# Reordered reloads, stored swapped spectra and moved bulk loads in a fused forward and backward kernel

## Chip, core and metric

The program runs on one NeuronCore of one Trainium2 chip. The metric is device microseconds for one execution of the whole program; the figure compared is the median of several executions.

## What is computed

A model of four residual layers, A, B, A, B, and all its gradients, for one sequence of S = 2048 positions and D = 448 channels in bf16:

```
x = A_q
x = x + A(layernorm(x), k, v, shift_k, ssm_k, ssm_D)
x = x + B(layernorm(x), w1, w2)
x = x + A(...)            # the same k, v, kernels
x = x + B(...)            # the same w1, w2

A(q, ...): k_shift = 4-tap causal convolution of k;  kv = k_shift * v
           y = irfft(rfft(kv, 4096) * rfft(ssm_k, 4096))[:2048] + kv * ssm_D
           return q * y
B(x, w1, w2): silu(x @ w1) @ w2,   w1 is 448 x 1792, w2 is 1792 x 448
```

The outputs are x and the gradients for q, k, v, shift_k, ssm_k, ssm_D, w1 and w2. Neither k, v nor the convolution kernels depend on x, so y is the same in both A layers and is computed once.

## The kernel before, in words

**Prefix** (`_ssm_prefix`). Two long transforms of length 4096, one of `ssm_k` and one of `kv`, are made as two stages of matrix products on TensorE: `_fft_stage1` with the constant M1 (128 x 16 x 2 x 128, 1 MB in bf16), transposes, then a second stage with the 128 x 128 constant `Gsb`. The real and imaginary parts of a spectrum lie in the two halves of the partitions (0 to 63 and 64 to 127). A complex product therefore needs two elementwise products: `pa` is spectrum times spectrum, `pb` is one spectrum times the other *with its halves swapped*. Both are then combined by TensorE with two constants (`GiA`, `GiB`, or their conjugate forms `GiAc`, `GiBc`). The two spectra are stored to DRAM as `SPEC_d["K"]` and `SPEC_d["KV"]` for the gradient.

**Main** (`Main.run`). The sequence is worked in four chunks c of 512 positions. Layers are numbered L = 0 (first B) and L = 1 (second B). The forward part runs chunk by chunk; each half of B's hidden layer (7 blocks of 128 features) is made by `h`. For L = 0, `h` stores the pre-activations to DRAM as `DT_d` and the activations, transposed, as `A_d[0]`. Four of the 14 feature blocks (`W2_PLAIN`) take another way: they go to DRAM as they are (`AP_d`), and `turn_plain(i)` later reads one block back through a transposing DMA and stores it.

- The *second loop over c for L = 1* does, for each chunk, `g_pre` (load and transpose the incoming gradient), the second half of `h`, `out`, then `ga`, and at the end `gn`.
- The *loop over c for L = 0* does the same backward part for the first B layer. Its silu slopes come from the stored pre-activations: `load_d(c, half)` reloads one 896 KB tile `dTl`, and `slope` turns it in place with ScalarE.
- `ga` makes, in seven steps `fp`, the product `ps_g` on TensorE, a copy `ghp` on ScalarE, and `ghT` = slope times `ghp` on VectorE. After step 3 the first half of `ghT` is complete, after step 6 the second: each is handed to `store_turned`, which issues two transposing DMAs and leaves the store to `GH_d` to the next call (`flush`).
- `gn` makes `ps_n` = `ghT` times w1 transposed and the backward of both layer norms, on VectorE for the greater part (`ln_bwd`). It writes `gYb`, the gradient of y.

All transposing DMAs, the reloads `dTl`, the loads `nb_l` and `na_l` (`load_n`) and the weight-gradient loads `dstat` are issued by SyncE (SP), in one queue and in order.

Buffers that matter: tag `D` has three slots for `dT` and `dTl`; a reload takes the slot that the `ghT` products just finished with. Tag `WA` holds w1 and later `GO` (the whole incoming gradient, 1.8 MB); tag `WB` holds w2 and later `mov3` (1.8 MB).

**Suffix** (`_ssm_suffix`). The transform of `gYb` (stage 1 with M1, reloaded as `M1s`; transposes into `Zg`), then seven pairs of chunks: `spectrum(cp)` makes the second stage for 2048 columns and loads the stored spectra `kk_c`; `inverse(cp)` makes `pa`, `pb` for both stored spectra and the inverse second stage `ps_v`. `spectrum(cp + 1)` is called before `inverse(cp)`. Then come the inverse first stage with `Minvs`, the elementwise products with `ksf` (the shifted k) and `gks` (v), and the gradients of k, v and the convolution kernels.

**Weight gradients** (`_gw2`, `_gw1`). 56 jobs: each loads a 512 KB tile `dstat` (from `A_d` or `GH_d`) and makes 16 matmuls `ps_d` against a moving matrix: `X`, `GO`, `mov3` or `mov1`. They stand last in the program.

**Order.** The framework's scheduler gives each engine one fixed order of instructions, made ahead from program order as priority, dependencies, buffer slots and a model of durations. Instructions that stand late in the program, the `ps_d` jobs above all, are put where the model finds an engine free. `issue_after(x)` keeps the instructions of a block behind x on their engine. On the chip each engine follows its order and waits on semaphores.

Of the kernel before, what the change touches and what calls it, by code (L numbers as in the profile page):

```python
# [13 lines left out]
ALU = mybir.AluOpType  # L14
# [19 lines left out]
def make_fft_consts():  # L34
# [44 lines left out]
    GiBc = np.roll(GiBc, 64, axis=0)  # L79
# [169 lines left out]
def _pm(ap2d):  # L249
    return ap2d.rearrange("(p j) d -> p j d", j=J)  # L250
# [213 lines left out]
class Main:  # L464
# [98 lines left out]
    def h(self, c, L, nT, half, hold):  # L563
# [3 lines left out]
        hold.append((aT, dT))  # L567
        for ft0, n, at in ((0, 2, 1), (2, 2, 0), (4, 2, None), (6, 1, None)) if half == 0 else ((7, 1, None), (8, 2, 1), (10, 2, 0), (12, 2, None)):
# [20 lines left out]
        if L == 1:  # L589
            self.store_turned(k.A_d[1], aT, c, half)  # L590

# [24 lines left out]
    def ga(self, c, L, gT, dT, mid=None):  # L616
        nc, k = self.nc, self.k
        ghT = [self.td.tile([P, NF // 2, 512], BF16, name=f"ghT{h}", tag="T", bufs=3) for h in range(2)]
        for fp in range(NF // 2):
# [12 lines left out]
            if fp in (3, 6):  # L632
                hh = (fp - 3) // 3
                self.store_turned(k.GH_d[L], ghT[hh], c, hh)
        return ghT
# [71 lines left out]
    def run(self):  # L707
# [21 lines left out]
        for c in range(4):  # L729
            gb, gT = self.g_pre(c, 1)  # L730
            self.h(c, 1, nT, 1, cur)
# [3 lines left out]
            self.turn_plain(c)  # L735
            if c == 3:
                d0 = self.load_d(0, 0)
                self.slope(d0)
                k.GO = k.wk.tile([P, NT, D], BF16, name="GO", tag="WA")
                with self.tc.issue_after(k.d_load.ins):  # L740
                    nc.sync.dma_start(out=k.GO[:], in_=_pm(k.grad_out[0]))
            box = []
            ghT = self.ga(c, 1, gT, cur, (lambda: box.append(self.b_pre(c + 1, 3))) if c < 3 else None)
# [5 lines left out]
            else:  # L749
                d1, e0 = self.load_d(0, 1), self.load_d(1, 0)  # L750
# [5 lines left out]
        for c in range(4):  # L756
# [3 lines left out]
            ghT = self.ga(c, 0, gT, dT, (lambda: self.slope(e0)) if c < 3 else None)  # L760
            if c < 3:
                d0, d1 = e0, self.load_d(c + 1, 1)
                if c < 2:
                    e0 = self.load_d(c + 2, 0)
                gn = self.g_pre(c + 1, 0)
            self.gn(c, 0, ghT, nb, lambda tl: self.X[:, 4 * c + tl, :], na)
            if c < 3:
                with self.tc.issue_after(k.d_load.ins):
                    nl = self.load_n(c + 1)
        self.flush()  # L770
# [53 lines left out]
def _ssm_suffix(k):  # L824
# [7 lines left out]
    with ExitStack() as es:  # L832
        pool = lambda name: es.enter_context(tc.tile_pool(name=name, bufs=1, reuse_waits="tile"))
        sp0 = pool("sp0")
        k.M1sb = sp0.tile([P, 16, 2, P], BF16, name="M1s", tag="kk0")
        with tc.high_priority():
            nc.gpsimd.dma_start(out=k.M1sb[:].rearrange("p a c k -> p (a c k)"), in_=k.m1_h.ap())
# [5 lines left out]
        k.mov3 = k.wk.tile([P, NT, D], BF16, name="mov3", tag="WB")  # L843
        ksf = k.yk.tile([P, J, D], BF16, name="ksf", tag="Y")
        B1k = A1[:].rearrange("p a c n s -> p (a c n s)").rearrange("p (q d) -> p q d", d=D)
        _load_minv(k, nc.gpsimd)
        for n2 in range(16):
            _fft_stage1(k, n2, k.gYb[:, n2, :], A1, psum)
        with tc.tile_pool(name="sspec2", bufs=1, reuse_waits="tile") as p1:
# [8 lines left out]
            def spectrum(cp):  # L858
                lo, hi = cp * 2048, (cp + 1) * 2048
                kk = (sp0.tile([P, 2, 2048], BF16, name="kk_c", tag="kk0") if cp % 2 else p1.tile([P, 2, 2048], BF16, name="kk_c", tag="kk1"))  # L860
                xsw = p1.tile([P, 2048], BF16, name="xsw_c", tag="xsw", bufs=2)
                t = [kk[:, 0, :], kk[:, 1, :], xsw]
                nc.gpsimd.dma_start(out=t[0], in_=k.SPEC_d["K"][:, lo:hi])
                nc.gpsimd.dma_start(out=t[1], in_=k.SPEC_d["KV"][:, lo:hi])
                if cp == 4:
                    nc.gpsimd.dma_start(out=k.mov3[:], in_=_pm(k.N_d[3][:]))
                if cp == 2:
                    nc.gpsimd.dma_start(out=ksf[:], in_=_pm(k.KS_d[:]))
# [6 lines left out]
                _swap_halves_dma(k, t[2], Zf, lo, hi, nc.scalar, dlo=0)  # L875
                return t

            def inverse(cp, t):
                for u in range(2):
                    ci = 2 * cp + u  # L880
                    o = slice(u * 1024, (u + 1) * 1024)
                    for spec_t, B1, cnd in ((t[1], B1k, True), (t[0], Z, False)):
# [148 lines left out]
```

## Time and profile before

| what | value |
|---|---|
| time, median of 3 runs | 791.22 us (789.21 to 795.2) |
| the profiled execution: time / span in the profile | 794.11 us / 792.3 us |
| TensorE (PE) busy | 724.7 us, 91% |
| VectorE (DVE) busy | 515.6 us, 65% |
| ScalarE (ACT) busy | 440.6 us, 56% |
| GpSimd (POOL) busy | 101.7 us, 13% |
| mean granted TensorE clock | 0.973 |
| DMA | 183.69 MB, mean 232 GB/s |

Stages by the trace: the prefix to about 100 us; the forward part and L = 1 backward to about 410; L = 0 backward (`dTl` slopes from 404) to 527 on TensorE and to about 550 on VectorE; the suffix's first stage from 532, its spectrum pairs from 568 to about 636; the remaining products to 784.

How to read the rows: PE is TensorE's matmuls, PEld its weight loads, SPq and POOLq the DMA-issuing queues. A row of the timeline is start, duration, engine, line, instruction, and in square brackets the idle time before it and what ended it. A DMA row's duration is that of its issue, not of its transfer. A row of the waits is the waiting instruction, what released it, and the total, number and longest of the waits. "idle" of an engine that isn't on the path costs nothing. In the tables of stretches the last three columns are granted clock, busy share of the DMA engines and GB/s.

### The profile page before, as it was taken

The page shows a single profiled execution, that of the slowest core. Times are in us where ns is not written, and L with a number is a line of the kernel's source. Part 1 is how long each engine was busy: PE and PEld are TensorE (multiplying, and loading weights), DVE is VectorE, ACT ScalarE, POOL GpSimd, SP SyncE. Part 2 cuts the span into 40 slices and gives each one's busy share as a digit, 9 for nine tenths or more (in the row PEclk, how much of TensorE's full clock was granted, in tenths as well). Part 3 has the DMA queues.
Part 4 walks back from the last instruction along what each step waited for, and adds up shares of the span by engine and source line. Part 5 has one row for each costly group of instructions (what it writes and reads, how often), then busy time and mean ns, then how long its engine had stood idle before and what let it go on. Part 6 is the DMA issues. An engine that isn't in the chain of part 4 may idle for free.

```text
span 792.3 us, 12745 instructions
## 1 busy us (share of the span) xinstructions
PE 724.7 (91%) x5025; PEld 381.3 (48%) x5025; DVE 515.6 (65%) x1056; ACT 440.6 (56%) x551; POOL 101.7 (13%) x169
## 2 busy tenths in 40 slices
PE   6999779999999999999978899996989998999995
PEld 4976534444444434434433343343556674545553
DVE  3789778788435978859457976985365625797110
ACT  4879867766466676876836866633536644000000
POOL 1133212222100010000000000010111022111111
PEclk9999989999999999999998999997989999999998
DMA  9359999999968869889998887995978766587660
GB/s 317 136 158 283 373 258 299 308 249 233 254 173 171 174 185 218 218 174 221 356 266 231 213 239 205 247 195 219 397 223 263 244 266 218 173 307 220 192 179 17
DMA packets 188888, 183.69 MB, mean 232 GB/s; under 512 B 135482, under 2 KB 164030, under 8 KB 187804
## 3 DMA queue, kind: packets, MB, share of 16 engines
q1 hardware_dynamic: 173664, 120.93, 59.2%
q0 software_dynamic: 12832, 53.92, 19.8%
q10 hardware_dynamic: 2332, 8.03, 3.2%
q8 instruction: 39, 0.64, 0.3%
q14 instruction: 21, 0.17, 0.1%
HBM read 76.50 MB, written 65.87 MB: 180 GB/s over the span
## 4 chain that ended last, share of the span: by engine, by line
PE 33%; DVE 21%; issue 20%; ACT 13%; DMA 8%; POOL 3%; SPq 0%; POOLq 0%; DVEq 0%; ACTq 0%
PE ps_h L518 5%; PE ps_d L778 5%; PE ps_o L598 4%; PE ps_g L518 4%; PE ps_n L666 3%; DVE dT L113 3%; DMA dTl<-DT_d 3%; ACT ghp L625 3%; DVE lb_junk L641 2%; DMA kk_c<-spec_KV 2%; DVE lb_u L652 2%; PE ps_v L232 2%; DVE ghT L630 2%; PE ps_v L233 2%; ACT na L274 2%
## 5 line engine op out<-in xcount | busy, mean ns | idle before, releaser
L778 PEld LDWEIGHTS <-dstat 128*128 128x128 bf16 x896 | 87.0, 99 | 87.4 <-issue 8.3
L518 PE MATMUL ps_g<-gT,w2T 128*128 128x512 bf16 (+1 forms) x448 | 100.7, 385 | 17.6 <-ACT ghp L625 17.0
L518 PE MATMUL ps_h<-nT,w1sb 128*128 128x512 bf16 (+1 forms) x448 | 103.9, 385 | 4.7 <-DVE dT L113 2.6
L666 PE MATMUL ps_n<-w1T,ghT 128*128 128x448 bf16 x448 | 94.2, 356 | 0.7 <-ACT lb_u L668 0.2
L598 PE MATMUL ps_o<-w2sb,aT 128*128 128x448 bf16 x448 | 90.8, 353 | 0.8 <-ACT aT L574 0.8
L778 PE MATMUL ps_d<-mov,dstat 128*128 128x448 bf16 x448 | 87.2, 352 | 0.9 <-DMA mov<-N_d 0.9
L574 ACT ACTIVATE aT<-ps_h 128x1024 bf16<-128x1024 f32 (+1 forms) x64 | 58.3, 917 | 37.6 <-PE ps_h L518 28.8
L113 DVE CAST dT<-ps_h 128x1024 bf16<-128x1024 f32 (+1 forms) x56 | 59.3, 1066 | 26.2 <-ACT aT L574 26.1
L518 PEld LDWEIGHTS <-w2T 128*128 128x128 bf16 (+1 forms) x448 | 36.3, 97 | 78.1 <-issue 47.3
L625 ACT CAST ghp<-ps_g 128x1024 bf16<-128x1024 f32 x56 | 56.5, 1008 | 30.6 <-DVE ghT L630 18.5
L518 PEld LDWEIGHTS <-w1sb 128*128 128x128 bf16 (+1 forms) x448 | 36.3, 97 | 68.3 <-issue 40.3
L666 PEld LDWEIGHTS <-ghT 128*128 128x128 bf16 x448 | 42.2, 98 | 45.4 <-issue 4.6
L598 PEld LDWEIGHTS <-aT 128*128 128x128 bf16 x448 | 42.1, 98 | 43.4 <-issue 4.3
L778 PE MATMUL ps_d<-X,dstat 128*128 128x448 bf16 x224 | 54.3, 372 | 5.1 <-DMA dstat<-A_d 5.1
L804 ACT COPY do<-ps_dt 112x512 bf16<-112x512 bf16 x14 | 8.2, 585 | 82.6 <-PE ps_dt L802 82.6
L232 PE MATMUL ps_v<-Gsb,pa 128*128 128x128 bf16 x336 | 43.2, 223 | 10.1 <-DVE Zg L113 5.8
L778 PE MATMUL ps_d<-GO,dstat 128*128 128x448 bf16 x224 | 50.0, 355 | 0.0
L233 PE MATMUL ps_v<-Gsb,pb 128*128 128x128 bf16 x336 | 42.2, 223 | 1.0 <-DVE pb L443 0.7
L819 DVE CAST dout<-ps_d 128x448 bf16<-128x448 f32 x14 | 8.7, 622 | 51.4 <-PE ps_d L778 51.4
L232 PEld LDWEIGHTS <-pa 128*128 128x128 bf16 x336 | 33.5, 100 | 11.7 <-DVE pa L442 6.3
L668 ACT ACTIVATE lb_u<-ps_n,rstd 128x448 f32<-128x448 f32 x32 | 20.2, 632 | 33.4 <-DVE X L653 12.1
L630 DVE TENSOR_TENSOR ghT<-dT,ghp 128x1024 bf16<-128x1024 bf16 (+1 forms) x32 | 19.5, 620 | 27.6 <-ACT ghp L625 27.6
(188 smaller groups left out, 1184.8 us busy)
## 6 DMA issues: line engine op xcount, KB each, us to landing
GH_d<-turned SPq DMA_DIRECT2D x16, 896.0 KB, 6.2
dstat<-A_d SPq DMA_DIRECT2D x28, 512.0 KB, 7.2
dstat<-GH_d SPq DMA_DIRECT2D x28, 512.0 KB, 3.8
A_d<-turned SPq DMA_DIRECT2D x12, 896.0 KB, 4.8
DT_d<-dT POOLq DMA_DIRECT2D x8, 896.0 KB, 6.3
dTl<-DT_d SPq DMA_DIRECT2D x8, 896.0 KB, 6.6
spec_K<-Z POOLq DMA_DIRECT2D x7, 512.0 KB, 7.5
KB<-Z POOLq DMA_DIRECT2D x14, 256.0 KB, 12.3
```

The costliest lines, as they stand in the source:

```text
L113: eng.tensor_copy(out, in_)
L232: nc.tensor.matmul(pv[:, i, :], lhsT=pa[:, i * P:(i + 1) * P], rhs=k.Gsb[:, ga, :], start=True, stop=False)
L233: nc.tensor.matmul(pv[:, i, :], lhsT=pb[:, i * P:(i + 1) * P], rhs=k.Gsb[:, gb, :], start=False, stop=True)
L274: nc.scalar.activation(n_g[:, tl, :], src(tl), ACT.Identity, bias=nmr[:, tl:tl + 1], scale=r[:, tl:tl + 1])
L518: self.nc.tensor.matmul(ps[:, u, :], lhsT=w[lo:hi, b, f:f + P], rhs=x[lo:hi, b, :], start=(seen[u] == 1), stop=(seen[u] == ND))
L574: last = nc.scalar.activation(a, ps[:, 0:n, :], ACT.Silu)
L598: nc.tensor.matmul(po[:, :D], lhsT=aT[ft // 7][0][:, ft % 7, tl * P:(tl + 1) * P], rhs=self.w2sb[:, ft, :], start=(ft == 0), stop=(ft == N ...
L625: k.last_gh = nc.scalar.copy(gh[:], ps[:])
L630: nc.vector.tensor_tensor(out=ghT[hh][:, o:o + len(u), :], in0=dT[hh][1][:, o:o + len(u), :], in1=gh[:, u[0]:u[0] + len(u), :], op=ALU.mult)
L666: nc.tensor.matmul(pn[:, :D], lhsT=ghT[ft // 7][:, ft % 7, tl * P:(tl + 1) * P], rhs=self.w1T[:, ft, :], start=(ft == 0), stop=(ft == NF - 1))
L668: last_u = nc.scalar.activation(u0[:], pn[:, :D], ACT.Identity, scale=k.rstd[2 * L + 1][:, t:t + 1], accum_out=cp[:, tl, 0:1])
L778: i = k.nc.tensor.matmul(ps[:, :D], lhsT=st[:, t, :], rhs=mov[:, t, :], start=start and t == 0, stop=stop and t == NT - 1)
```

## The change

Main. The reloads of pre-activations move ahead of transposes on SP's queue: `d0` is loaded at the start of the last `h` of L = 1, and `ga` takes a pair `loads`, of which each is issued just before `store_turned` of its half. Two plain turns each are made in c = 0 and 1, none in c = 2 and 3. `GO` is loaded at the end of c = 0 of the last loop instead of in c = 3 of the loop before. `M1s` is loaded by SP in c = 2 of the last loop, into w2's buffer, instead of by GpSimd into a pool of the suffix at its beginning.

Suffix. The halves are no longer swapped on the fresh spectrum `Zg` (two DMAs from ScalarE's queue per pair, after the second stage's copies). Instead each stored spectrum is loaded twice, once as it is and once with its halves swapped, six DMAs from GpSimd's queue per pair, into a tile of four instead of two parts with two slots. The row rotation of the constant `GiBc` that undid the other swap is dropped. `Minvs`, `ksf` and `gks` are loaded behind the second pair's spectra, `mov3` behind the last pair's.

```
-    GiBc = np.roll(GiBc, 64, axis=0)

-    def h(self, c, L, nT, half, hold):
+    def h(self, c, L, nT, half, hold, pre=None):
...
         hold.append((aT, dT))
+        d0 = pre() if pre else None
...
+        return d0

-    def ga(self, c, L, gT, dT, mid=None):
+    def ga(self, c, L, gT, dT, mid=None, loads=(None, None)):
         nc, k = self.nc, self.k
+        ld = []
...
             if fp in (3, 6):
                 hh = (fp - 3) // 3
+                if loads[hh]:
+                    ld.append(self.load_d(*loads[hh]))
                 self.store_turned(k.GH_d[L], ghT[hh], c, hh)
-        return ghT
+        return (ghT, *ld) if ld else ghT

# run, second loop over c (L = 1)
-            self.h(c, 1, nT, 1, cur)
+            d0 = self.h(c, 1, nT, 1, cur, (lambda: self.load_d(0, 0)) if c == 3 else None)
...
-            self.turn_plain(c)
+            if c < 2:
+                self.turn_plain(2 * c)
+                self.turn_plain(2 * c + 1)
             if c == 3:
-                d0 = self.load_d(0, 0)
                 self.slope(d0)
-                k.GO = k.wk.tile([P, NT, D], BF16, name="GO", tag="WA")
-                with self.tc.issue_after(k.d_load.ins):
-                    nc.sync.dma_start(out=k.GO[:], in_=_pm(k.grad_out[0]))
...
+            if c < 3:
+                ghT = self.ga(c, 1, gT, cur, lambda: box.append(self.b_pre(c + 1, 3)))
+            else:
+                ghT, d1, e0 = self.ga(c, 1, gT, cur, None, ((0, 1), (1, 0)))
...
-                d1, e0 = self.load_d(0, 1), self.load_d(1, 0)
+                k.GO = k.wk.tile([P, NT, D], BF16, name="GO", tag="WA")
                 k.go_jobs = k.d_load

# run, last loop over c (L = 0)
-            ghT = self.ga(c, 0, gT, dT, (lambda: self.slope(e0)) if c < 3 else None)
+            ghT = self.ga(c, 0, gT, dT, (lambda: self.slope(e0)) if c < 3 else None, ((c + 1, 1) if c < 3 else None, (c + 2, 0) if c < 2 else None))
             if c < 3:
-                d0, d1 = e0, self.load_d(c + 1, 1)
-                if c < 2:
-                    e0 = self.load_d(c + 2, 0)
+                d0, (ghT, d1, *e) = e0, ghT
+                e0 = e[0] if e else None
...
                 with self.tc.issue_after(k.d_load.ins):
                     nl = self.load_n(c + 1)
+                    if c == 0:
+                        nc.sync.dma_start(out=k.GO[:], in_=_pm(k.grad_out[0]))
+                    if c == 2:
+                        k.M1sb = k.wk.tile([P, 16, 2, P], BF16, name="M1s", tag="WB")
+                        nc.sync.dma_start(out=k.M1sb[:].rearrange("p a c k -> p (a c k)"), in_=k.m1_h.ap())

# suffix
-        sp0 = pool("sp0")
-        k.M1sb = sp0.tile([P, 16, 2, P], BF16, name="M1s", tag="kk0")
-        with tc.high_priority():
-            nc.gpsimd.dma_start(out=k.M1sb[:].rearrange("p a c k -> p (a c k)"), in_=k.m1_h.ap())
...
-        _load_minv(k, nc.gpsimd)
...
-                kk = (sp0.tile([P, 2, 2048], BF16, name="kk_c", tag="kk0") if cp % 2 else p1.tile([P, 2, 2048], BF16, name="kk_c", tag="kk1"))
-                xsw = p1.tile([P, 2048], BF16, name="xsw_c", tag="xsw", bufs=2)
-                t = [kk[:, 0, :], kk[:, 1, :], xsw]
-                nc.gpsimd.dma_start(out=t[0], in_=k.SPEC_d["K"][:, lo:hi])
-                nc.gpsimd.dma_start(out=t[1], in_=k.SPEC_d["KV"][:, lo:hi])
-                if cp == 4:
-                    nc.gpsimd.dma_start(out=k.mov3[:], in_=_pm(k.N_d[3][:]))
-                if cp == 2:
-                    nc.gpsimd.dma_start(out=ksf[:], in_=_pm(k.KS_d[:]))
+                t = p1.tile([P, 4, 2048], BF16, name="kk_c", tag="kk", bufs=2)
+                for i, nm in enumerate(("K", "KV")):
+                    nc.gpsimd.dma_start(out=t[:, i, :], in_=k.SPEC_d[nm][:, lo:hi])
+                    kv = _swap_halves_dma(k, t[:, 2 + i, :], k.SPEC_d[nm], lo, hi, nc.gpsimd, dlo=0)
+                with tc.issue_after(kv.ins):
+                    if cp == 1:
+                        _load_minv(k, nc.gpsimd)
+                        nc.gpsimd.dma_start(out=ksf[:], in_=_pm(k.KS_d[:]))
+                        nc.gpsimd.dma_start(out=gks[:], in_=v_pm)
+                    if cp == NCI // 2 - 1:
+                        nc.gpsimd.dma_start(out=k.mov3[:], in_=_pm(k.N_d[3][:]))
...
-                _swap_halves_dma(k, t[2], Zf, lo, hi, nc.scalar, dlo=0)
...
-                        nc.vector.tensor_tensor(out=pb[:], in0=t[2][:, o], in1=spec_t[:, o], op=ALU.mult)
+                        nc.vector.tensor_tensor(out=pb[:], in0=Zf[:, ci * 1024:(ci + 1) * 1024], in1=t[:, 2 + i, o], op=ALU.mult)
...
-        for h in range(2):
-            sl = slice(8 * h, 8 * h + 8)
-            nc.scalar.dma_start(out=gks[:, sl, :], in_=v_pm[:, sl, :])
```

More of the change, by code (lines that the diff above doesn't have):

```diff
@@ L734, in run @@
             self.out(c, cur, True)
-            self.turn_plain(c)
+            if c < 2:
+                self.turn_plain(2 * c)
+                self.turn_plain(2 * c + 1)
             if c == 3:
-                d0 = self.load_d(0, 0)
                 self.slope(d0)
-                k.GO = k.wk.tile([P, NT, D], BF16, name="GO", tag="WA")
-                with self.tc.issue_after(k.d_load.ins):
-                    nc.sync.dma_start(out=k.GO[:], in_=_pm(k.grad_out[0]))
             box = []
-            ghT = self.ga(c, 1, gT, cur, (lambda: box.append(self.b_pre(c + 1, 3))) if c < 3 else None)
+            if c < 3:
+                ghT = self.ga(c, 1, gT, cur, lambda: box.append(self.b_pre(c + 1, 3)))
+            else:
+                ghT, d1, e0 = self.ga(c, 1, gT, cur, None, ((0, 1), (1, 0)))
             cur = []
@@ L842, in _ssm_suffix @@
         Z = sp.tile([P, NDH, P], BF16, name="Zg")
-        k.mov3 = k.wk.tile([P, NT, D], BF16, name="mov3", tag="WB")
         ksf = k.yk.tile([P, J, D], BF16, name="ksf", tag="Y")
         B1k = A1[:].rearrange("p a c n s -> p (a c n s)").rearrange("p (q d) -> p q d", d=D)
-        _load_minv(k, nc.gpsimd)
         for n2 in range(16):
@@ L881, in inverse @@
                     o = slice(u * 1024, (u + 1) * 1024)
-                    for spec_t, B1, cnd in ((t[1], B1k, True), (t[0], Z, False)):
+                    for i, B1, cnd in ((1, B1k, True), (0, Z, False)):
                         pa = p1.tile([P, 1024], BF16, name="pa", tag="pa", bufs=3)
                         pb = p1.tile([P, 1024], BF16, name="pb", tag="pb", bufs=3)
-                        nc.vector.tensor_tensor(out=pa[:], in0=Zf[:, ci * 1024:(ci + 1) * 1024], in1=spec_t[:, o], op=ALU.mult)
-                        nc.vector.tensor_tensor(out=pb[:], in0=t[2][:, o], in1=spec_t[:, o], op=ALU.mult)
+                        nc.vector.tensor_tensor(out=pa[:], in0=Zf[:, ci * 1024:(ci + 1) * 1024], in1=t[:, i, o], op=ALU.mult)
+                        nc.vector.tensor_tensor(out=pb[:], in0=Zf[:, ci * 1024:(ci + 1) * 1024], in1=t[:, 2 + i, o], op=ALU.mult)
                         bal.add("dve", 1.38)
                         _fft_inv_stage2_chunk(k, pa, pb, True, B1, ci, psum, cnd=cnd)
+            gks = k.xg.tile([P, J, D], BF16, name="gks", tag="GY")
+            k.mov3 = k.wk.tile([P, NT, D], BF16, name="mov3", tag="WB")
             prev = spectrum(0)
@@ L896, in _ssm_suffix @@
         p2 = es.enter_context(tc.tile_pool(name="sp2", bufs=1, reuse_waits="tile"))
-        gks = k.xg.tile([P, J, D], BF16, name="gks", tag="GY")
         gkh = p2.tile([P, 3, D], BF16, name="gkh")
```

## The prediction, made before the change was run

> **What bounds the kernel now.** I read four views in turn: the page's busy shares, TensorE's waits, the timelines around the three longest of them, and busy time by stretch.
>
> ```profile
> span 792.3 us, 12745 instructions
> PE 724.7 (91%) x5025; PEld 381.3 (48%) x5025; DVE 515.6 (65%) x1056; ACT 440.6 (56%) x551; POOL 101.7 (13%) x169
> ```
>
> TensorE is busy 91% and the change takes no large matmul away. So the time is TensorE's work plus its holes, and a hole closed anywhere is worth its length, because the weight-gradient products `ps_d` fill TensorE to the end (the stretches from 580 us on are over 97% busy). The question is which holes go and which come. TensorE's waits from 400 to 580 us:
>
> ```profile
> PE ps_g L518 <- ACT ghp L625: 14.4, 7, 8.3
> PE ps_v L232 <- DVE Zg L113: 5.3, 1, 5.3
> PE ps_d L778 <- DMA dstat<-A_d: 5.1, 1, 5.1
> PE ps_s L212 <- ACT A1g L111: 1.8, 1, 1.8
> ```
>
> Columns: total, times, longest. In 30-us stretches TensorE's idle time is 8.3, 3.5, 2.4, 0.9, 7.1 and 5.4 us from 400 to 580, 27.6 in sum, and 0.7 from 580 to 640. First hole, the SP queue and the ScalarE rows it holds up:
>
> ```profile
> 389.67 9.62 SPq L484 DMA_TRANSPOSE turned<-ghT  x2
> 399.38 0.53 SPq L690 DMA_DIRECT2D dTl<-DT_d  x1
> 401.44 0.37 SPq L486 DMA_DIRECT2D GH_d<-turned  x1
> 401.90 7.20 SPq L484 DMA_TRANSPOSE turned<-ghT  x2
> 409.19 0.80 SPq L690 DMA_DIRECT2D dTl<-DT_d  x1
> ...
> 415.27 1.06 ACT L560 ACTIVATE dTl<-dTl 128x1024 bf16<-128x1024 bf16 x1 [7.46 <-DMA dTl<-DT_d]
> ...
> 418.84 3.23 PE L518 MATMUL ps_g<-gT,w2T 128*128 128x512 bf16 x8 [8.27 <-ACT ghp L625]
> ```
>
> The reload e0 is issued at 409.19, after 7.2 us of issuing two transposes that it doesn't need. ScalarE stands in order at its slope, the `ghp` copies stand behind it, TensorE behind them. The suffix's hole:
>
> ```profile
> 550.36 0.54 POOL L868 DMA_DIRECT2D ksf<-KS_d  x1 [10.91 <-DVE lb_u L681]
> ...
> 557.82 1.08 POOL L863 DMA_DIRECT2D kk_c<-spec_K  x2 [0.94 <-PE ps_s L212]
> 558.88 1.05 POOL L864 DMA_DIRECT2D kk_c<-spec_KV  x2
> ...
> 575.40 1.29 DVE L885 TENSOR_TENSOR pa<-Zg,kk_c 128x1024 bf16<-128x1024 bf16 x2 [5.68 <-DMA kk_c<-spec_KV]
> ...
> 581.77 1.90 DVE L886 TENSOR_TENSOR pb<-xsw_c,kk_c 128x1024 bf16<-128x1024 bf16 x3 [3.34 <-DMA xsw_c<-Zg]
> ```
>
> The first spectra wait for M1s's slot (last ps_s), [...]need 16 us. The reader is also to see what a hole costs after it ends:
>
> ```profile
> 416.00:420.00 4.00, 1.16 (x3) 0.40 (x3) 3.02 (x7) 4.00 (x7) 0.00 (x0) 0.50 1.04 407
> ...
> 544.00:548.00 4.00, 4.00 (x12) 1.66 (x11) 2.63 (x4) 0.91 (x1) 0.00 (x0) 0.50 0.04 14
> ...
> 576.00:580.00 4.00, 2.12 (x7) 1.07 (x8) 2.43 (x4) 0.00 (x0) 0.00 (x0) 0.50 0.88 223
> ```
>
> First TensorE's busy time, and in the third column from the right the granted clock: half, after each long hole. Busy time x (1 - clock) over the 4-us stretches gives 1.5 us lost after the first hole (416 to 424), 1.7 at 480 to 484, 3.2 at 536 to 548, 2.2 at 576 to 584.
>
> [...]so an SP queue held up by transposes holds all behind it, as 401.90 to 409.19 shows. [...]between 555 and 580 the trace has 40.2, 30.4 and 28.3% on three queues, 369 GB/s together.[...]
>
> **The change, part by part.**
>
> *A, e0 before the second half's transposes (ga at c = 3).* Its slot is free with VectorE's last product (398.47 + 0.69 = 399.2). d1, now ahead of the first half's transposes, adds its 0.53 us to the queue, so SP is free at 399.9 and e0 lands 6.1 to 7.1 us later, at 406 to 407. ScalarE wants it when slope(d1) ends (404.35 + 3.47 = 407.8). The 7.46 us wait goes, and with a hole under 1 us so do the 1.5 us of slow clock: 9.0. The transposes go out half a microsecond later, and their store is only read by the last products, after 680 us. I take 8.5.
>
> *B, the same in the second loop, c = 0 and 1.* e0 is issued at 439.59 and 470.15, behind 7.5 and 8.5 us of transposes, and ScalarE waits 1.97 and 2.00 us; TensorE's holes there are 2.51 and 1.96. Issued 7 us earlier they are in time. 4.5; the clock's 1.7 at 480 is left as margin. Next in line is VectorE: 23 to 24.5 us busy of each 30.
>
> *C, the seam at 527 to 548.* M1 (1.0 MB at 519.47) moves to SP at about 500 us and Minv (1.0 MB at 527.70) behind the spectra. Both ran beside the last transposes, which took 9.71 us to issue (518.24) and let their store go only at 535.04; only then came the dstat load that TensorE missed for 5.1 us. 2.1 MB less at the 369 GB/s above is some 5.7 us of the engines, part of it in that window. The hole and its clock are 8.3 us with ps_s's 1.8 beside; between nothing and 9, I take 4.
>
> *D, the first spectra.* Without M1s in their slot, and with ksf behind instead of ahead, they can be issued after the last G store (553.9) instead of 557.8. Now it is six issues of 0.53 us and 2.1 MB, 3.2 us, and the last lands some 8 us on (spec_KV's median is 8.5), at 565 to 567; the Zg chain wants them at 570. The hole (5.3) and its clock (2.2) go: 7.5, taken as 6.5 because the spectra of the second pair run on the same queue.
>
> *E, doubled spectra and 4.7 MB of bulk.* Against it: each pair now loads 2.1 MB instead of 1.05 from memory, and the 0.52 MB swap from Zg goes, with ScalarE's 14 issues (0.5 to 0.6 us each, 7.5 us) and VectorE's 11.5 us of waits for xsw_c, both hidden by ps_d today. Per period (8.8 us in the timeline) 0.52 MB more is 60 GB/s on the 238 measured from 580 to 610; the trace shows over 400, so the steady state holds. The start doesn't: Minv, ksf and gks (4.7 MB) stand on POOL's queue between the second pair and the third. 2.1 + 2.1 + 4.7 MB at about 260 GB/s (369 less 105 for dstat, five 0.52 MB loads from 555 to 580) lasts from 554 to 588, and the third pair lands at 596 where it is wanted at 571 + 2 x 8.7 = 588. 8 us late if no ps_d stands in the gap; VectorE's lead over TensorE (2 to 3 us, an estimate from its 2 to 3 us waits that cost nothing) takes some off, half clock afterwards adds about as much. Bounds: 0 (products fill it) to -32 (rival 4); I take -8.
>
> *F, the rest.* Plain turns go from c = 2, 3 to c = 0, 1: 2 to 3 us of issue on SP each, in a stretch where SP waits for aT and ghT anyway; if that cover went, at most the next transposes' 3 us. GO (1.8 MB at 375) goes to the end of c = 0, about 440, and is first read at 503; mov3 goes from 382.6 to the last pair, about 615, and is read at 694; either is hidden by 60 us of products. The d0 reload goes ahead of h: ScalarE's 1.35 us wait at 372 goes, but an earlier slope among Silu calls may add table loads (1.28 us each, at 373.34 and 375.67): -3 to +2, I take +0.5. Rolling the constant costs nothing on the chip.
>
> Sum: 8.5 + 4.5 + 4 + 6.5 + 0.5 - 8 = 16 us. The profiled execution took 794.1 us (span 792.3), so 778; it stands 2.9 above the median of 791.2, which gives 775.
>
> **Rivals.**
> 1. *Forecast, 775* (766 to 783): A and D have one clear late transfer each.
> 2. *VectorE takes the holes' place in the loop.* At 24 of 30 us with in-order chains of layer-norm work, A and B keep 6 of 13: 782. For it: c = 2 to 3 has no reload wait and yet 27.8 us from transposes to transposes. Against: the 8.3 us hole is a plain halt of ScalarE.
> 3. *The suffix gives it back.* E is -23, by a late third pair (8), 3 us in each of four later pairs (12) and slow clock (3): 790. For it: the order on TensorE is fixed ahead, so a late pair stops ps_d too. Against: xsw_c's waits have stopped nothing.
> 4. *Slower.* One mechanism: with two buffers a pair's period is at least (products + landing) / 2. Products are 8 x 0.61 = 4.9 us; if 2.1 MB needs the 19 us that spec_KV needed at 558, the period is 12 instead of 8.8: 6 x 3.2 = 19, with the late third pair 8 and half clock after the holes 5, -32 against the +24 of A to D and F: 799. It puts the time above before's from 16 us of landing on (period 10.6). Against: later spectra landed in 7 to 9 us for half the bytes.
>
> **How the numbers follow.** Chances: forecast 0.55, VectorE 0.16, giving back 0.15, slower 0.14. About 1% (8 us) is what can be told from no change. Faster by more: all of 1, 0.11 of 2, 0.02 of 3, together 0.68. Within 1%: 0.05 of 2, 0.10 of 3, 0.01 of 4, together 0.16. Slower: 0.03 of 3, 0.13 of 4, together 0.16. The range runs from 762 (A to D in full, E at about half its loss) to 794, which leaves out most of 4 and the worst of 3.
>
> **What would show it.** Right: dTl issued just before each pair of ghT transposes; no ScalarE wait of over 1 us for dTl near 405; kk_c issued from 554 less what the loop saved, and no VectorE wait for it at the first product; TensorE's idle time from 400 to 580 near 10 us. Wrong: a hole of over 5 us at the third pair with kk_c named as releaser, or pairs over 10 us apart (E), or ps_g holes released by ghT or lb_ rows of VectorE (2). The forecast fails if the spectra's landing exceeds 15 us throughout.

## The result: slower by 3.4%, and the profile after

The changed kernel takes 818.88 us (median of 4 runs, 815.39 to 822.17) against 792.3 us for the kernel before (789.21 to 795.2): a ratio of 1.0335, 95% interval 1.0276 to 1.0395. The forecast of 775 us had the wrong sign. The profiled execution took 819.3 us, its span is 817.4. In the experiments below the times are medians of all runs and the ratios leave out slow runs, those over 1.5% above the fastest of the same kernel, which are eight of 21 in e1 and nine of 20 in e7 (whose median is 782.04 us without them).

The page of the changed kernel, the same two lines as shown of before:

```profile
span 817.4 us, 12726 instructions
PE 733.0 (90%) x5025; PEld 389.3 (48%) x5025; DVE 516.2 (63%) x1056; ACT 440.7 (54%) x551; POOL 117.8 (14%) x197
```

TensorE runs the same 5025 matmuls, but they take 8.3 us longer (724.7 before). Most of that is granted clock, lost after holes: busy time x (1 - clock), summed over 4-us stretches as in the prediction, gives 19.1 us, and 12.2 before. The other 16.8 of the 25.1 us of span are idle time, 84.4 us instead of 67.6. Busy time by stretch of the changed kernel (start and end, length, then busy time of PE, PEld, DVE, ACT, POOL, granted clock, DMA share, GB/s):

```profile
400.00:540.00 140.00, 128.15 (x649) 56.86 (x648) 114.49 (x305) 88.58 (x128) 2.71 (x5) 0.96 0.94 249
540.00:700.00 160.00, 129.07 (x1267) 85.44 (x1266) 78.51 (x133) 60.53 (x66) 42.82 (x76) 0.91 0.84 242
```

Length less PE busy, for before, after and the last experiment, e13, all at the same microseconds:

| stretch | idle before | idle after | idle in e13 |
|---|---|---|---|
| 0 to 400 | 27.8 | 28.6 | 25.2 |
| 400 to 540 (last loop) | 19.9 | 11.9 | 9.2 |
| 540 to 700 (suffix) | 11.5 | 30.9 | 16.0 |
| 700 to the end | 8.5 | 13.1 | 10.3 |

The last loop gains 8 us; the suffix loses 19 and the clock. TensorE's waits in the changed kernel (total, times, longest), and VectorE's behind them:

```profile
PE ps_g L517 <- ACT ghp L627: 12.9, 15, 5.4
PE ps_v L231 <- DVE pa L889: 11.8, 7, 3.7
PE ps_v L232 <- DVE pb L890: 8.1, 5, 3.3
...
DVE pa L889 <- DMA kk_c<-spec_KV: 28.7, 4, 13.4
```

**The suffix.** `ps_v`, which before had one long wait of 5.3 us for the end of `Zg`, now waits again and again for products, and the products wait for the stored spectra. The timeline of VectorE has the first products of pairs 1 to 4:

```profile
557.05 1.89 DVE L889 TENSOR_TENSOR pa<-Zg,kk_c 128x1024 bf16<-128x1024 bf16 x3
...
569.67 1.90 DVE L889 TENSOR_TENSOR pa<-Zg,kk_c 128x1024 bf16<-128x1024 bf16 x3 [6.82 <-DMA kk_c<-spec_KV]
...
595.74 1.89 DVE L889 TENSOR_TENSOR pa<-Zg,kk_c 128x1024 bf16<-128x1024 bf16 x3 [13.39 <-DMA kk_c<-spec_KV]
...
609.40 1.90 DVE L889 TENSOR_TENSOR pa<-Zg,kk_c 128x1024 bf16<-128x1024 bf16 x3 [5.76 <-DMA kk_c<-spec_KV]
```

The first product comes at 557.05, 18.3 us sooner than before, and without a wait. Then pair follows pair after 12.6, 26.1 and 13.7 us. First to last product is 84.9 us; before it was 60.6. How the DMA engines worked meanwhile, in 4-us stretches:

```profile
576.00:580.00 4.00, 3.93 (x57) 3.18 (x55) 1.29 (x2) 3.49 (x4) 0.44 (x1) 1.00 0.98 412
...
592.00:596.00 4.00, 1.20 (x7) 0.39 (x4) 0.26 (x1) 0.00 (x0) 0.59 (x2) 1.00 1.02 268
...
608.00:612.00 4.00, 0.46 (x2) 0.19 (x2) 1.90 (x3) 1.14 (x2) 0.54 (x2) 0.94 1.04 219
612.00:616.00 4.00, 2.83 (x27) 2.83 (x28) 3.01 (x5) 1.01 (x1) 0.00 (x0) 0.50 1.00 216
```

Read the last two columns together. The engines are busy all the time in each of these rows, yet they move 412 GB/s while the bulk loads (whole 128 partitions; `ksf` lands at 579, `gks` at 585) run and 216 to 268 while spectra do. Over all full-share stretches from 552 to 568 and from 584 to 636 it is 216 to 289. A full share at 216 of 412 GB/s, little more than half the rate, means that the transfers themselves are slow here. The experiments ask why. The third column from the right is the clock, half again after the hole at 608.

**The loop.** SyncE's queue does what the change says at c = 3 (the reload `dTl` for e0 is issued at 401.21 instead of 409.19), and yet most of the first hole is there:

```profile
393.56 7.55 SPq L483 DMA_TRANSPOSE turned<-ghT  x2
401.21 0.52 SPq L694 DMA_DIRECT2D dTl<-DT_d  x1
...
407.65 1.06 ACT L559 ACTIVATE dTl<-dTl 128x1024 bf16<-128x1024 bf16 x1 [6.81 <-DMA dTl<-DT_d]
408.61 0.62 ACT L672 ACTIVATE lb_u<-ps_n,rstd 128x448 f32<-128x448 f32 x1
...
409.22 4.41 ACT L559 ACTIVATE dTl<-dTl 128x1024 bf16<-128x1024 bf16 x5
...
416.65 5.13 PE L517 MATMUL ps_g<-gT,w2T 128*128 128x512 bf16 x16 [5.39 <-ACT ghp L627]
```

The slope that waits at 407.65 is that of e0. It now stands ahead of `lb_u` at 408.61, and so ahead of d1's slope, which is kept behind that `lb_u` by `issue_after`: the earlier reload pulled its own consumer forward in ScalarE's fixed order, and all of d1's slope, on which TensorE's `ps_g` depends, came behind a transfer that it didn't need.

### The profile page after: what moved, and what is told of

It reads as the page before. It is cut to its first block, busy times and chain, and to the rows that moved or that the text cites. A ratio compares the mean times of both kernels' runs of the same rounds, so it can differ in the third digit from the quotient of the medians.

```text
span 817.4 us, 12726 instructions
## 1 busy us (share of the span) xinstructions
PE 733.0 (90%) x5025; PEld 389.3 (48%) x5025; DVE 516.2 (63%) x1056; ACT 440.7 (54%) x551; POOL 117.8 (14%) x197
## 4 chain that ended last, share of the span: by engine, by line
issue 42%; PE 20%; DVE 12%; DMA 12%; ACT 9%; POOL 4%; ACTq 0%; POOLq 0%; SPq 0%; DVEq 0%
DMA kk_c<-spec_KV 8%; PE ps_o L599 5%; PE ps_h L517 5%; DVE dT L112 3%; ACT na L273 2%; DVE ln_st L259 1%; DMA KB<-Z 1%; POOL out_dram L814 1%; PE ps_v L232 1%; PE ps_cv L369 1%; DMA K_sb<-in_A_ssm_k_dram 1%; PE ps_v L231 1%; ACT aT L574 1%; POOL rstd L266 1%; PE ps_d L787 1%
## 5 line engine op out<-in xcount | busy, mean ns | idle before, releaser
L670 PE MATMUL ps_n<-w1T,ghT 128*128 128x448 bf16 x448 | 92.3, 353 | 0.5 <-DVE ghT L632 0.2
L574 ACT ACTIVATE aT<-ps_h 128x1024 bf16<-128x1024 f32 (+1 forms) x64 | 58.4, 918 | 39.6 <-PE ps_h L517 30.9
L231 PE MATMUL ps_v<-Gsb,pa 128*128 128x128 bf16 x336 | 51.4, 242 | 18.7 <-DVE pa L889 11.8
L232 PE MATMUL ps_v<-Gsb,pb 128*128 128x128 bf16 x336 | 48.4, 243 | 9.3 <-DVE pb L890 8.1
L787 PE MATMUL ps_d<-X,dstat 128*128 128x448 bf16 x224 | 50.3, 358 | 0.0
L231 PEld LDWEIGHTS <-pa 128*128 128x128 bf16 x336 | 37.0, 110 | 23.7 <-DVE pa L889 15.7
L232 PEld LDWEIGHTS <-pb 128*128 128x128 bf16 x336 | 36.5, 111 | 16.2 <-DVE pb L890 9.9
L889 DVE TENSOR_TENSOR pa<-Zg,kk_c 128x1024 bf16<-128x1024 bf16 x28 | 18.2, 687 | 38.6 <-DMA kk_c<-spec_KV 28.7
```

The costliest lines, as they stand in the source:

```text
L231: nc.tensor.matmul(pv[:, i, :], lhsT=pa[:, i * P:(i + 1) * P], rhs=k.Gsb[:, ga, :], start=True, stop=False)
L232: nc.tensor.matmul(pv[:, i, :], lhsT=pb[:, i * P:(i + 1) * P], rhs=k.Gsb[:, gb, :], start=False, stop=True)
L574: last = nc.scalar.activation(a, ps[:, 0:n, :], ACT.Silu)
L670: nc.tensor.matmul(pn[:, :D], lhsT=ghT[ft // 7][:, ft % 7, tl * P:(tl + 1) * P], rhs=self.w1T[:, ft, :], start=(ft == 0), stop=(ft == NF - 1))
L787: i = k.nc.tensor.matmul(ps[:, :D], lhsT=st[:, t, :], rhs=mov[:, t, :], start=start and t == 0, stop=stop and t == NT - 1)
L889: nc.vector.tensor_tensor(out=pa[:], in0=Zf[:, ci * 1024:(ci + 1) * 1024], in1=t[:, i, o], op=ALU.mult)
```

## Experiments

Ratios are to the kernel before, run on the same chip in the same batch.

| kernel | us | ratio, 95% interval |
|---|---|---|
| the change | 818.88 | 1.0335 (1.0276 to 1.0395) |
| e1 loop alone | 789.66 | 0.9958 (0.993 to 0.9986) |
| e2 suffix alone | 816.49 | 1.0313 (1.0262 to 1.0364) |
| e3 bulk loads as before | 816.09 | 1.0312 (1.0254 to 1.037) |
| e4 whole-row loads | 788.02 | 0.9968 (0.9942 to 0.9994) |
| e5 e3 and e4 | 790.98 | 1.0003 (0.998 to 1.0027) |
| e6 192 rows, copied early | 843.72 | 1.0573 (1.0456 to 1.069) |
| e7 e1 and slope order | 787.43 | 0.9902 (0.987 to 0.9933) |
| e8 before, loads in halves | 802.84 | 1.0127 (1.0049 to 1.0205) |
| e9 pieces by columns | 789.09 | 0.9962 (0.9941 to 0.9983) |
| e10 192 rows, stored twice | 812.5 | 1.0244 (1.02 to 1.0288) |
| e11 e7 and the seam | 798.54 | 1.0074 (1.0043 to 1.0105) |
| e12 e11, bulk behind | 795.2 | 1.0083 (1.0053 to 1.0114) |
| e13 192 rows, copied late | 786.38 | 0.9934 (0.9909 to 0.9959) |

### Which part costs: e1 and e2

Each takes one half of the change. e1 has the reloads, the plain turns and GO, with M1 and the suffix of before; e2 the reverse, with M1 loaded by SyncE.

> The kernel before with the reloads, the plain turns and GO moved as in the change; M1 and the whole suffix as before. In the changed kernel VectorE's last G store of the loop came 8.5 us sooner (545.4 against 553.9). Theory 1 (the loop gains, the suffix loses more): 780 to 785. Rival (the seam's gain came from M1 and the spectra, not from the reloads): 788 to 792.

> The kernel before with the changed suffix and M1 loaded early into w2's buffer; reloads, turns and GO as before. Theory 1: the loss is all in the suffix, so this is slower than the changed kernel by what the loop gained, 824 to 830. Rival (the two parts hurt each other through the order on the queues): under 812.

789.66 and 816.49: neither came where its first theory had it. e1 lies in its rival's range and e2 between its two. The loss is the suffix's (ratio 1.0313 of 1.0335), and the loop alone is worth 0.4%, not the 13 us that parts A and B claimed.

### Bulk loads or half-partition loads: e3, e4, e5

Two theories for the late pairs. A: the 4.7 MB of `Minvs`, `ksf` and `gks` between the second pair and the third. B: the swapped tiles, each loaded in two pieces of 64 partitions. e3 puts the bulk where before had it, e4 replaces the two pieces by one load of the same bytes into 128 partitions (the swapped order is left out, so the gradients of k and v are not the reference's), e5 does both.

```
# e4
-    kv = _swap_halves_dma(k, t[:, 2 + i, :], k.SPEC_d[nm], lo, hi, nc.gpsimd, dlo=0)
+    kv = nc.gpsimd.dma_start(out=t[:, 2 + i, :], in_=k.SPEC_d[nm][:, lo:hi])
# e3
+        _load_minv(k, nc.gpsimd)                               # ahead of stage 1
+        nc.gpsimd.dma_start(out=ksf[:], in_=_pm(k.KS_d[:]))
...
+            nc.scalar.dma_start(out=gks[:, sl, :], in_=v_pm[:, sl, :])   # after the pairs
```

> The changed kernel with Minv and ksf issued ahead of the spectra and gks again by ScalarE's queue in two halves; all spectra loads as in the change. Theory A (the 4.7 MB of bulk between the second and the third pair is the cause): the 26 us between the second and the third pair's first products fall to under 12, time 797 to 803. Theory B (the loads of swapped halves are slow in themselves): pairs stay 9 to 13 us apart, the third is only half as late, 808 to 816.

> The changed kernel with each pair of half-swapping loads replaced by one load of the same 512 KB over all 128 partitions, not swapped (so the conjugate products are taken with the wrong halves: the gradients of k, v and their kernels are not the reference's). Same bytes, four instead of six issues a pair, bulk where the change put it. Theory B (64-partition loads run at half the rate, 216 to 265 GB/s at full DMA share from 588 to 612): landing falls to under 10 us and the time to 796 to 803. Theory A (bulk): no better than 812.

> Both of the last two edits: whole 128-partition loads in place of the swapping halves (again not swapped, so the gradients of k, v and their kernels are not the reference's) and Minv and ksf ahead of the spectra, gks by ScalarE's queue. With whole rows and the bulk in the change's place the third pair was still 20 us behind the second (558.7 to 578.7), but products filled it. If the bulk costs once the halves are gone: 778 to 783. If it is hidden by products: 786 to 790.

e3: 816.09, no gain. Its third pair is no longer late (592.87, after 581.04), but the first is (570.76), and all follow some 10.5 us apart. Its stretches show the same low rate, with no bulk beside it:

```profile
604.00:608.00 4.00, 1.47 (x11) 1.11 (x12) 3.54 (x6) 0.00 (x0) 0.52 (x1) 0.56 1.05 241
612.00:616.00 4.00, 2.15 (x19) 1.00 (x16) 0.99 (x2) 3.64 (x4) 1.60 (x4) 1.00 1.02 227
```

e4: 788.02, 31 us less than the change and less than either theory had, from four loads per pair in place of six and no byte fewer. Two stretches of e4 at a DMA share of about 1:

```profile
600.00:604.00 4.00, 2.70 (x24) 1.52 (x23) 3.93 (x6) 1.56 (x3) 1.37 (x3) 1.00 0.98 379
604.00:608.00 4.00, 3.08 (x49) 2.84 (x49) 3.72 (x7) 2.92 (x4) 0.00 (x0) 1.00 1.04 433
```

The median from issue to landing of all spectra loads falls from 11.8 us to 7.7. e5 (790.98) is no faster than e4, near what it expected of a bulk that products hide: with whole loads, the third pair still waits 10.6 us for the bulk in e4, but TensorE has other products then (18.3 of 20 us busy from 560 to 580). Theory A is refuted as the cause of the time; B stands, with one gap: e4 changed the number of loads too.

### Number of loads or shape: e8 and e9

GpSimd's queue in the change shows each DMA from 552.72 to 569.86 waiting on the one eight before it, 0.41 to 3.23 us each (the issue at 552.72 waits 1.66 us for the load issued at 546.79), so six loads per pair could be the cost rather than their shape. e9 keeps six and cuts the swapped tile by columns (the swapped order is again left out). e8 goes the other way: the kernel before, with each of its spectrum loads cut into two of 64 partitions, unswapped.

```
# e9
+    for x in (0, 1024):
+        kv = nc.gpsimd.dma_start(out=t[:, 2 + i, x:x + 1024], in_=k.SPEC_d[nm][:, lo + x:lo + x + 1024])
# e8, in the kernel before
+    for i, nm in enumerate(("K", "KV")):
+        for a in (0, 64):
+            nc.gpsimd.dma_start(out=t[i][a:a + 64], in_=k.SPEC_d[nm][a:a + 64, lo:hi])
```

> The whole change, but each swapped tile is loaded as two pieces cut by columns (128 partitions by 1,024 values) where the change has two pieces cut by rows (64 partitions by 2,048); six loads of spectra for each pair on GpSimd's queue, as in the change, with the same bytes. The swapped order of rows is left out, so the gradients of k and v are not the reference's. If loads into half of the partitions are what is slow: about 788 us as with whole rows, not over 796, and 340 GB/s or more while the DMA share is at 1. If it is the number of loads (six for a pair and three tiles' worth of others on a queue that keeps eight under way): 811 to 820 us, as with the change.

> The kernel before, with each 512 KB spectrum load cut into two loads of 64 partitions each, not swapped: same bytes, same data, four issues in place of two. Theory B: [...]landing rises from 7.4 and 8.5 us to 10 to 13, and the time rises by 3 to 12 us, since pairs 8.8 us apart leave little slack. If cutting a load costs only its issue: within 2 us of before.

e9: 789.09, within 0.1% of e4. In its stretches the engines are at full share with 380 and 403 GB/s:

```profile
588.00:592.00 4.00, 2.54 (x35) 1.86 (x33) 3.61 (x6) 2.03 (x3) 0.80 (x2) 1.00 1.01 380
...
608.00:612.00 4.00, 2.97 (x47) 2.61 (x45) 4.00 (x8) 2.62 (x4) 0.00 (x0) 1.00 0.97 403
```

So the number of loads is not it. Same bytes, same six issues, same queue: pieces of 64 partitions 818.88, pieces of 128 partitions 789.09, although the rows of the latter are half as long. e8 has as many half-loads as the change, four per pair, but half the bytes per pair. It loses 1.3%, and its trace shows where: VectorE waits 14.1 us in all for spectra (6.0 before), and TensorE 9.0 us at the first product (5.3 before).

```profile
DVE pa L886 <- DMA kk_c<-spec_KV: 14.1, 5, 9.4
...
PE ps_v L232 <- DVE Zg L113: 12.0, 3, 9.0
```

The time is in the expected range, the landing isn't: its median is 7.3 us, not 10 to 13. But each of e8's loads carries half the bytes of before's, which land in 7.7. That the half rate hurts at the crowded start and little later is read from the waits above (9.4 of the 14.1 us are one wait), not tested.

### ScalarE's order: e7

e1 with the slope of e0 kept behind the middle `lb_u`, as d1's slope already was.

```
+    def slope_e(self, d):
+        with self.tc.issue_after(self.k.mid_u.ins):
+            self.slope(d)
...
-    ghT = self.ga(c, 0, gT, dT, (lambda: self.slope(e0)) if c < 3 else None, ...
+    ghT = self.ga(c, 0, gT, dT, (lambda: self.slope_e(e0)) if c < 3 else None, ...
```

> The loop-only kernel, with the slope of e0 in the last loop kept behind the middle lb_u on ScalarE, as d1's is. In the changed kernel the first quarter of slope(e0) had come to stand on ScalarE ahead of d1's slope and of that lb_u, and waited 6.8 us for its reload. Theory: that new order used up the gain of the earlier reload; here TensorE's hole at 410 falls from 5.4 us (8.4 in the loop-only kernel's profile) to under 2 and the time from 787 to 779 to 783. Rival (the hole is set by the layer-norm chain on VectorE): the hole stays above 4 us and the time at 786 to 789.

787.43; the ratio goes from 0.9958 to 0.9902, and the two intervals only just overlap. TensorE's first hole is 4.21 us (8.27 before, 5.39 in the change):

```profile
409.07 1.06 ACT L560 ACTIVATE dTl<-dTl 128x1024 bf16<-128x1024 bf16 x1 [3.63 <-DMA dTl<-DT_d]
...
413.58 5.65 PE L518 MATMUL ps_g<-gT,w2T 128*128 128x512 bf16 x16 [4.21 <-ACT ghp L632]
```

The expected hole of under 2 us was missed, and 787.43 is in the rival's range. The rival's cause, the layer-norm chain on VectorE, is not what the rows show, though: a slope still waits 3.63 us for its reload, which SyncE issues at 402.62, now with d1's four slopes ahead of it (401.99). e7 has the lowest ratio of all the kernels here; by the median of all runs e13 is lower (786.38).

### A swapped tile in one load, everything computed: e6 and e10

If rows 0 to 63 stand in memory a second time, as rows 128 to 191, then rows 64 to 191 are the swapped spectrum and one load fills all partitions. e6 makes the second set by a copy within memory, with the bulk as in e3; e10 stores it from SBUF in the prefix, with the change's bulk and e7's slope.

```
+    k.SPEC_d = {nm: dram.tile([192, SPEC], ...
+    kv = nc.gpsimd.dma_start(out=t[:, 2 + i, :], in_=k.SPEC_d[nm][64:192, lo:hi])
# e6, second loop, c = 0 and 1
+    nc.gpsimd.dma_start(out=k.SPEC_d[nm][128:192, :], in_=k.SPEC_d[nm][0:64, :])
# e10, beside each store of the prefix
+    nc.gpsimd.dma_start(out=k.SPEC_d["K"][128:192, lo:hi], in_=Ka[0:64, lo:hi])
```

> The swap done by storage: each spectrum lies in DRAM with 192 rows, rows 128 to 191 a copy of rows 0 to 63 made by one DMA in the second loop, and the swapped tile is one whole load of rows 64 to 191; Minv and ksf ahead, gks by ScalarE's queue. Complete computation. Theory B (the halves' rate is the cause): as fast as the kernel with whole, unswapped loads and the bulk away, within 4 us. If reading rows from row 64 on, or the copies, cost by themselves: over 800.

> The whole computation: the prefix stores rows 0 to 63 of each spectrum a second time, from SBUF, as rows 128 to 191 (14 more stores of 256 KB), so that a swapped tile is one load of rows 64 to 191 into all partitions; the slope of the next half in the last loop is kept behind the middle products on ScalarE; else as the change. If half-partition loads were the loss and the order on ScalarE the rest: 788 with whole rows, less the 4 to 5 us that the order gave, and 0 to 8 for the stores in the prefix: 783 to 791 us. If the second set of rows is as dear wherever it is written (the copy within DRAM cost some 40 us at 150 to 190): over 800.

Both miss the first range by far and lie in the second: 843.72 and 812.5. But it isn't the loads from row 64. e10's suffix is as quick as hoped (577.96 to 636.6, 58.6 us), its time goes elsewhere. SyncE's queue in e10:

```profile
128.72 19.23 SPq L503 DMA_TRANSPOSE w1T<-in_B_w_dram  x1
148.06 15.62 SPq L485 DMA_TRANSPOSE turned<-aT  x1
163.80 0.52 SPq L714 DMA_DIRECT2D x0c<-in_A_q_dram  x1
```

In the kernel before these rows are 6.66 us at 110.43, 3.79 at 117.19, and `x0c` at 121.09. The spectra's stores on GpSimd's queue, twice as many, are issued up to 109.42 (before, up to 92.02); before, SyncE waits 8.0 us in all for such stores ahead of its first weight transpose, which goes out at 102.92, in e10 at 119.32. The two transposes above then take three to four times as long to issue, beside stores of `DT_d` (127.01, 136.71, 145.93) that before began only behind `w1T` (119.06). What slows them, these stores or something else, was not taken apart. `x0c` stands behind them, and VectorE's layer norm waits for it:

```profile
168.00 0.63 DVE L259 BATCH_NORM_STATS2 ln_st<-x0c 128x6 f32<-128x448 bf16 x1 [19.70 <-DMA x0c<-in_A_q_dram]
```

TensorE's longest wait there, for a copy behind that layer norm, is 19.5 us. In e6 the scheduler had set the two copies (1.8 MB each) far ahead of the second loop, at 90.86 and 103.80. The second took 39.1 us to land, and the two transposes of w2 beside it took 30.21 and 28.30 us to issue (5.59 and 1.82 before).

### The same, copied at another time: e13

```
# loop L = 1, after gn; k.x_store is the store of X in out()
+    with self.tc.issue_after(k.x_store.ins):
+        for cp in range(2 * c, min(2 * c + 2, 7)):
+            for nm in ("K", "KV"):
+                nc.gpsimd.dma_start(out=k.SPEC_d[nm][128:192, 2048 * cp:2048 * cp + 2048],
+                                    in_=k.SPEC_d[nm][0:64, 2048 * cp:2048 * cp + 2048])
```

> The whole computation and the whole change (M1 early, large loads behind the third pair's spectra), with each swapped tile as one load of rows 64 to 191, as in the two kernels with 192 rows; but the second set of rows is copied within DRAM in the third loop, two or four copies of 256 KB at a time behind the four stores of X at about 233, 282, 332 and 384, and not while the weights are transposed at 103 to 150; the slope of the next half behind the middle products. If half-partition loads are what made the change slower, and the weights' transposes what made the two 192-row kernels slower: 780 to 788 us, ratio 0.985 to 0.997, and no idle stretch at 140 to 200. If 192 rows, or loads from row 64, are dear in themselves: over 800.

786.38, ratio 0.9934, inside the range of the first theory (the large loads stand behind the second pair's spectra, as in the change). The weight transposes are back at their old length and the copies land in about 5.1 us. A row of SyncE's timeline and one of TensorE's:

```profile
110.87 6.66 SPq L501 DMA_TRANSPOSE w1T<-in_B_w_dram  x1
...
411.01 1.78 PE L517 MATMUL ps_g<-gT,w2T 128*128 128x512 bf16 x8 [0.92 <-ACT ghp L631]
```

The second row is the first hole: 8.27 us before, 0.92 here. And the stretch in which the change was at 279 GB/s, with TensorE busy 13.66 us of 20:

```profile
580.00:600.00 20.00, 18.78 (x225) 13.89 (x224) 14.25 (x24) 16.36 (x17) 7.79 (x15) 1.00 0.96 363
```

This is the whole change with two things mended, the shape of the swapped loads and the order of one slope. Loads from row 64 are not dear in themselves. It beats the kernel before by 0.7% and the change by 32 us.

### The seam alone: e11 and e12

e7 with M1 loaded by SyncE in the last loop, fresh spectrum swapped as before; e12 also puts `ksf`, `gks` and `mov3` behind spectra of the third, fourth and last pair.

```
# both
+    k.M1sb = k.wk.tile([P, 16, 2, P], BF16, name="M1s", tag="WB")      # c = 2, by SyncE
-    k.M1sb = sp0.tile([P, 16, 2, P], BF16, name="M1s", tag="kk0")
# e12, in spectrum(cp)
+    with tc.issue_after(kv.ins):
+        if cp == 2: nc.gpsimd.dma_start(out=ksf[:], in_=_pm(k.KS_d[:]))
+        if cp == 3: nc.gpsimd.dma_start(out=gks[:], in_=v_pm)
```

> The loop's new order with the slope behind the middle products, the suffix's products as before (fresh spectrum swapped), and of the change's seam only this: M1 is loaded by SyncE in the last loop, into the buffer of the sums, not by GpSimd into a tile of the spectra. If the seam is worth what part C said: 4 us under the 787.4 of the loop's order alone, ratio near 0.985 to before. If the products would only wait at the next place (stored spectra land no sooner, or the swap is the last to come): no gain, ratio 0.990.

> As the seam alone (new loop order, slope behind the middle products, M1 loaded by SyncE in the last loop, fresh spectrum swapped as before), but the three large loads (ksf, v, the fourth moving tile) are issued on GpSimd behind the spectra of the third, fourth and last pair. If the seam alone lost because M1 took the buffer of the fourth moving tile, whose 1.8 MB then came with ksf and v ahead of the spectra: no wait of 18 us for a spectrum, first product at 551 to 560, and 779 to 785 us (ratio 0.983 to 0.991). If what is won at the first product is given back in the pairs, as with whole rows: 0.990 to 0.997.

798.54 and 795.2 with e7 at 787.43: the seam alone is a loss of 1.7% by the ratios, and both expectations for e12 were missed. In e11's order `mov3` (1.8 MB, which shares its buffer with M1) had moved from before the last loop (382.62) to 559.20, just ahead of the spectra issued at 559.80. e12 takes that away and gains nothing by its ratio: now the swap of the fresh spectrum, `xsw_c`, stands behind the bulk. VectorE's rows in e12:

```profile
585.76 0.69 DVE L903 TENSOR_TENSOR pb<-xsw_c,kk_c 128x1024 bf16<-128x1024 bf16 x1 [8.98 <-DMA xsw_c<-Zg]
...
628.12 0.69 DVE L903 TENSOR_TENSOR pb<-xsw_c,kk_c 128x1024 bf16<-128x1024 bf16 x1 [8.31 <-DMA xsw_c<-Zg]
```

`gks` was issued at 576.77 and `mov3` at 612.04, each with a swap needed next. Stage 1 of e12 also starts 6.0 us late on TensorE, behind the last transposes (ScalarE waits 7.2 us for `turned<-ghT`), which e13 doesn't show. Why M1 early makes those transposes end later here and not there was not settled.

## Why the prediction was wrong, point by point

**E, the step that failed.** It read "the trace shows over 400, so the steady state holds". The 400 was measured on loads almost all into 128 partitions (399 to 426 GB/s in the four 4-us stretches from 560 to 576 before); half of the new bytes go into 64 at a time. At full DMA share the engines then move 216 to 289 GB/s. By an estimate from these rates, and from e9's 380, a pair's 2.1 MB take some 8.7 us of all engines (at 240 GB/s) instead of about 5.5 (at 380), with `dstat`, the bulk and the stores still to come. The prediction booked the swapped loads at the rate of whole tiles; the missing term is the rate of a load into 64 partitions. The lowest full-share stretches of the change show 216 and 219 GB/s, the others up to 289. Why such a load is slower, no run here shows. E was booked at -8. Measured from 540 to 700, with D's gain in it, are 19.4 us more idle time, and 5.5 of the 8.3 us of longer busy time are slow clock there (10.7 us lost, 5.2 before).

**Its bulk.** The third pair was predicted 8 us late because of 4.7 MB; it waited 13.39, so the mechanism is there. But it isn't what costs the time: with whole loads it waits 10.6 us (e4) and TensorE works on, and without the bulk the halves cost the same 816 (e3).

**A, right mechanism, wrong size.** 8.5 booked, 2.9 gained (hole 8.27 to 5.39). The working followed e0 through SyncE's queue and took ScalarE's order as unchanged. "Of a step that moves, ask what its consumer does in the fixed order" was the missing question. With the consumer held back e7 has a hole of 4.21 and e13 one of 0.92, 7.4 us gained; in e13 the reload also leaves SyncE 2.7 us sooner than in e7 (399.89 against 402.62), so the slope's order is not all of it.

**B happened once in two.** 4.5 booked. At c = 0 the reload is issued at 432.15 instead of 439.59, and TensorE's hole of 2.51 us is gone. At c = 1 it is issued at 464.75, sooner than the 470.15 of before but after 10.04 us of two transposes; ScalarE waits 2.99 us for it, and the hole is 2.96 us instead of 1.96. Idle time from 440 to 480 went from 5.66 to 5.07. The scheduler set the transposes of the two halves around the loads in its own way, and the program's order was not the queue's.

**C and D closed their holes, and it didn't help.** C: idle from 520 to 560 fell from 7.09 to 0.88 (4 booked). D: the first product comes 18.3 us sooner, without a wait. But D's gap of 5.3 us is followed by one of 3.69 us at the second pair in the change. And in e13, where the halves are mended and the first product is at 550.31, 25 us sooner than before, the suffix has 4.5 us more idle time than before, not less.

So a premise failed too: "a hole closed anywhere is worth its length", because `ps_d` fills TensorE to the end. It rested on stretches that are "over 97% busy" from 580 on. That is the mean to 780 (97.9%); from 640 to 660 it is 91%. And the fixed order has `ps_d` only where the scheduler put it. From the first product to the last, before and in the change, it is busy for:

```profile
575.40:636.00 60.60, 31.67 (x135) 0.00 (x0) 2.19 (x4) 0.94 0.75 233
...
557.00:642.00 85.00, 23.58 (x106) 0.00 (x0) 1.08 (x2) 0.86 1.01 282
```

In the change the last of these start at 592.8: nothing stands in the gaps that follow. In e13 TensorE has 7.2 us of `ps_d` from 600 to 640 (18.9 before) and waits 5.0 us for `gK` behind the pairs (1.7 before). That the place of the filler is what takes the gain back is read from these traces; no run moved it. What e13 keeps is the loop's 10.7 us (19.9 to 9.2), less the suffix's 4.5 and 1.8 at the end. 2.6 came before 400, where the copies, the plain turns, the d0 reload and `GO` differ; which of them it is, is not shown.

**F** was booked at +0.5. Idle time to 400 changed by 0.8 the other way; nothing here tests it further.

**Rivals.** Rival 4 had the sign. Its 799 us were still 20 short: it set -32 for the suffix against +24 from the rest, where the measured change has 19.4 us more idle time in the suffix, 4.6 at the end and 8.3 us of longer busy time against 8.0 from the loop. Its term was off too: it asked for 19 us of landing throughout and set its point at 16, and the prediction's last sign of failure was a landing of over 15 throughout. The median is 11.8, the last pairs follow 9 us apart (618.23, 627.49, 636.22), and the loss is made in the first four. Its argument against, that later spectra land in 7 to 9 us for half the bytes, was again a whole-load number. Rival 2 was not tested by itself; in e13 the ScalarE rows around the first hole wait for VectorE's `ghT` (up to 1.54 us each). But the longest hole left in that loop, 3.65 us at 470.37 behind ScalarE's `ghp`, looks like a late reload again: SyncE issues it at 459.99, after 11.37 us of two transposes, much as in the change (464.75 after 10.04). The list of signs named the right ones: a hole of over 5 us at the third pair with `kk_c` as releaser, and pairs over 10 us apart.

## What to carry to other kernels

Before a rate is used for a new transfer, look at which partitions it fills: bytes and number of loads can stay, and a cut by rows of 64 instead of by columns made 30 us of difference here. When an issue is moved forward, follow its consumer too, because an order fixed ahead may pull it forward with it and set it in front of work that was ready. And an idle stretch that is closed by starting a stage earlier can come back later, where the fixed order has no filler: sum TensorE's idle time over the whole rest of the span, not at the hole.

## What was not expected of the hardware

- In this suffix DMA share and rate together tell the shape of the transfers: at a share of about 1.0, 216 to 289 GB/s in the change with its half-partition loads, 379 to 433 with the same bytes into all partitions (the 4-us stretches of e4 and e9 shown above, from 588 to 612; e13 has 412 from 560 to 580). A low rate at full share isn't a mark of halves alone, though: from 520 to 540 before, with two transposes issued from 518.24 on and no half-partition load, it is 237 GB/s at a share of 1.04.
- The issue of a transposing DMA has no fixed length. That of `w1T` took 6.66 us before and in e13, 19.23 in e10; those of w2's halves took 5.59 and 1.82 before, 30.21 and 28.30 in e6 beside a copy within memory. In e10 TensorE then waits 19.5 us, for a copy behind the layer norm that waits for `x0c`, and the kernel takes 26 us more than e13. The 14 copies of 256 KB spread over 234 to 386 in e13 cost nothing that can be seen: TensorE's idle time to 400 is 25.2 us there and 27.8 before.
